# A gated mix of attention and linear attention: the thresholds of its list scheduler set by a table, one row for eight score passes

## The chip, the cores and the metric

The kernel runs on one core of one Trainium2 chip. The metric is device time of one launch in microseconds (us). Before the change it is 669.52 us, the median of 3 runs (669.35 to 669.65).

## What is computed

For 2048 tokens of 512 columns, the reference forms two attention results from the same input `x` and mixes them with a gate per token:

```python
x = A_x                                                     # 1 x 2048 x 512
g = _sigmoid((x * gate_w).sum(-1, keepdims=True))
# A: softmax attention, 32 heads of 16
scores = jnp.einsum("bhqd,bhkd->bhqk", q, k) * (Dh ** -0.5)
p = _softmax(scores, axis=-1)
o = jnp.einsum("bhqk,bhkd->bhqd", p, v)                     # then @ wo
# B: linear attention, 32 heads of 16
phi = lambda t: jnp.where(t > 0, t + 1, jnp.exp(t)) + 1e-6
pq, pk = phi(q), phi(k)
kv = jnp.einsum("bhsd,bhse->bhde", pk, v)
z = jnp.einsum("bhsd->bhd", pk)
o = num / den                                               # num = pq kv, den = pq z + 1e-6; then @ wo
return g * a + (1 - g) * b
```

The large part is the softmax of A: 32 heads x 2048 x 2048 exponentials.

## The kernel before, in words

**Units and rounds.** The scores are worked off in 32 rounds. A round is eight heads (one of four groups, `t8`), 512 query columns (`qc`) and one half of the heads (four, `j` = 0 to 3, in four strips of 32 rows of the TensorE array). A unit is one block of 128 keys for one head, a matmul into one PSUM bank of 128x512. A round has 16 x 4 = 64 units, the kernel 2048.

**Two ways for an exponential.** Most units go to ScalarE (ACT): one ACTIVATE (L2075) takes the two or three neighbouring banks of a *score pass* and writes weights to `PT`. The passes alternate between banks 0 to 2 and 3 to 5. The other units are *claimed* for VectorE (DVE): one TENSOR_SCALAR (L1569, in `claim`) turns a score bank into the integer bits of an approximate exponential in `DP`. Four claimed units make a group, and for the group two shifted copies are made by integer additions (L1613 on POOL, or L1610 on DVE when that comes earlier). The three versions are weighted by three scaled copies of the values, so a claimed unit needs three products with the values, a unit on ACT one. A claimed unit's score bank is the third bank of a pass, the third bank of the other half, or bank 7.

**The other work.** Projections of keys, values and queries for the next head group, the linear branch B (its `phi` is made by ACT at L974 and two DVE operations at L977 and L979, in `phi_post`), the gate, and the output projection are cut into *steps* of a few matmuls each. The steps wait in chains (`a_chain`, `b_chain`, `e_chain` for the start, `o_chain` for the output) with a target pass. Steps use bank 7 or the bank that isn't the accumulator (bank 6 and 7 change roles), and in a few cases a *lent* third bank of the ring. The last rounds, normalisation and final stores stand at the end.

**The order.** Nothing is decided on the chip. When the program is built, Python code simulates the engines with assumed durations (`PE.t`, `AC.t`, `DV.t`, `PO.t`) and puts instructions on each engine's list in the order in which it decides them; semaphores follow from what reads and writes what. The main loop makes one pass `g` after the other (L1988 on):

- it looks for free banks (`more`), picks two or three units for ACT and up to two claims (`extras`), and emits their score matmuls as one group and the ACTIVATE;
- until the banks of the next pass are read (`t_lim`), it fills TensorE's time: sets of products with the values (`pv_step`, up to `MOST` sets), chain steps (`misc_step`), and else filling matmuls on zeros (`fill`), which keep TensorE's clock up;
- `t_late` is the last moment at which TensorE may be busy before ACT would wait for scores: `AC.t` less the length of a score group and `MARGIN`;
- DVE's operations are queued as items with a priority (`push`), and `pump` emits the best of them: those whose wait is short come first, then by priority (0 ahead of 1), then by possible start.

The thresholds in these rules are constants: `WAIT3` (how long TensorE waits for the third bank), `WAIT_M` (for bank 7), `RING_LOAD` (up to which queue on DVE a claim is made), `TWO_LOAD` and `THIRDS` (a third ACT unit or a second claim), `OVER` and `FIRST_T` (how far a step may run over `t_late`), `MOST`, `ROOM`, `LEAST`, `PV_LAG` and `PT_URGENT` (products: how many sets, and when those of `PT` go first), `MIN_LEFT`, `ALONE`, `MOST_OPEN` (claims), `POOL_WAIT`, `WAIT_BANK` and `LOOK` (choices in `pump`), and a few more.

**Lending.** If steps are far behind or `e_chain` isn't empty, and no bank is free, the head of a chain is chosen at the start of a pass (`lend = due`, a pair of step and chain). After the pass's scores are emitted, the chain's head is popped and the chosen step is started on the pass's own third bank, where the pass has two units.

Of the kernel before, what the change touches and what calls it, by code (L numbers as in the profile page):

```python
# [19 lines left out]
HIST = {}  # L20
SLOTS = [(0, 3), (3, 3)]
# [193 lines left out]
def bass_gated_mix__mha_block__linear_attn_block__prompt_kernel(  # L215
# [33 lines left out]
    with ExitStack() as es:  # L249
# [164 lines left out]

        items = []
# [22 lines left out]
        POOL_WAIT = 0.7  # L438
# [124 lines left out]

        WAIT_BANK = 0.12
# [6 lines left out]
        def pump(now, look=0.25):  # L571
            try_close()
            pool_go()
            while items and DV.t <= now + look:
                best = None
                for it in items:
# [3 lines left out]
                    if len(o) > 6 and not due_now(it) and PO.t < DV.t + POOL_WAIT:  # L580
# [3 lines left out]
                    key = (wait > (WAIT_BANK if it.prio <= 1 else 0.12), -1 if it is boost[0] else it.prio, st, it.seq)  # L584
# [4 lines left out]
                if best[2] > now + look + WAIT_BANK:  # L589
                    return  # L590
# [379 lines left out]
        def phi_post(b, dst, dres):  # L970
# [5 lines left out]
            push(1, [  # L976
# [360 lines left out]
        PT_URGENT = 12  # L1337

# [4 lines left out]
        def pv_cols(now, r, force, want, most, least):  # L1343

            urgent = sum(1 for e in pv_pending if e[3] in r_PT) > PT_URGENT
# [84 lines left out]
        def pv_step(now, force=False, want=None, most=3, least=4):  # L1430
# [25 lines left out]
            elif sum(1 for e in pv_pending if e[3] in r_PT) > PT_URGENT:  # L1456
# [54 lines left out]
        def claim_round():  # L1511
# [4 lines left out]
            if left(r) >= (MIN_LEFT_LAST if last else MIN_LEFT):  # L1516
                return r
# [3 lines left out]

        MIN_LEFT = 14
        MIN_LEFT_LAST = 20

        def can_claim(now, js):
# [14 lines left out]
            if not try_close() and len(closing) > MOST_OPEN and (tri[0] is None or len(tri[0][1]) == NTRI - 1):  # L1540
                return None
# [14 lines left out]
        def claim(r, u, b, beside, in_group=False):  # L1556
# [12 lines left out]
            push(0 if in_group else 1, [(lambda: nc.vector.tensor_scalar(DP[:, i, 512 * k:512 * (k + 1)].bitcast(I16),  # L1569
# [18 lines left out]
        MOST_OPEN = 1  # L1588
# [137 lines left out]
        def due_step(now):  # L1726
            load = dve_load(now)
            due = None
            for ch in chains:
# [3 lines left out]
                if (st.target > cur_g[0] and not hurry()) or not step_ready(st, now):  # L1733
                    continue
# [13 lines left out]
        def second_claim(c, now, js):  # L1748
# [7 lines left out]
            elif len(tri[0][1]) == NTRI - 2 and len(closing) > MOST_OPEN:  # L1756
                return None
            if left(r) < 3 + MIN_LEFT:
# [10 lines left out]
        def misc_step(now, t_late):  # L1769

            if hold[0] is not None:
                if now + (SWITCH_T if pe_mode[0] == "full" else 0.0) + hold[0][2][0][2] > t_late + OVER:
# [6 lines left out]
            if b is None:  # L1779
# [3 lines left out]
                if due is None or due[0].keeps or now + FIRST_T > t_late + OVER:  # L1783
                    return False
                b3 = next((b for b in (2, 5) if is_free(b, now)), None)
                if b3 is None or not is_free(7 - b3, t_late + WAIT3):
# [6 lines left out]
            c = can_claim(now, (0, 1, 2, 3)) if ALONE and load < CLAIM_LOAD else None  # L1793
            if due is not None and (c is None or load > STARVE or cur_g[0] > due[0].target + late() or hurry()):
                if now + FIRST_T > t_late + OVER:
# [28 lines left out]

        WAIT3 = 0.05
        WAIT_M = 0.1
        THIRDS = 1
        LATE_M = 100
        TWO_LOAD = 4
        ALONE = 0  # L1830
# [4 lines left out]
        MOST = 4  # L1835
        OVER = 0.15
        FIRST_T = 0.43
        ROOM = 0.6
        CLAIM_LOAD = 3.2
        LATE_CLAIM = 4  # L1840
        STARVE = 5
# [5 lines left out]
        RING_LOAD = 4  # L1847
# [4 lines left out]
        MARGIN = 0.19  # L1852
        PV_LAG = 14
# [138 lines left out]
        while True:  # L1992
            us = []
# [11 lines left out]
            if g > last_stage:  # L2005
                soon = PE.t + WAIT3
                more = [b for b in (b0 + 2, 7 - (b0 + 2)) if is_free(b, soon)][:THIRDS]
                due = due_step(PE.t)[0] if hold[0] is None else None
                if not reserved() and hold[0] is None and (due is None or cur_g[0] <= due[0].target + LATE_M):
                    eb = bank_free(PE.t + WAIT_M)  # L2010
                    if eb is not None:
                        more.append(eb)
            while len(us) < SLOTS[g % 2][1]:
                if len(us) == 2 and (away or lend is not None):
                    break
                if len(us) == 2 and g > last_stage:
                    own, j3 = b0 + 2 in more, peek()
                    load = dve_load(PE.t)
                    if more and load < (RING_LATE if behind_by() > BEHIND else RING_LOAD):
                        js = [j for j in range(4) if j not in [u % 4 for _, u in us]]  # L2020
                        three = own and len(more) > 1 and load >= TWO_LOAD and j3 in js
# [7 lines left out]
                        elif c is not None:  # L2029
                            extras = [(c, more[1 if three else 0])]  # L2030
# [336 lines left out]
```

## Time and profile before

| | |
|---|---|
| median of 3 runs | 669.52 us (669.35 to 669.65) |
| profiled execution: its time, its span | 669.31 us, 667.5 us |
| granted TensorE clock, mean | 0.999 |
| exponentials of A on ACT: passes of 2 units, of 3 units | 626, 44 |
| claimed units on DVE | 664 |
| integer additions on POOL, on DVE | 320, 12 |

The span reaches from the first to the last instruction; the time of a run is a little longer. In the page's lines a group of instructions is named by its line, engine, operation and tiles, with its count, its busy time and mean duration, and the idle time of its engine just before it with what ended that idle time. A row of a stretch lists its limits and length, and then busy time with the instruction count in brackets for PE, weight loads, DVE, ACT and POOL, the granted clock, the DMA share and GB/s.

### The profile page before, as it was taken

The page shows a single profiled execution, that of the slowest core. Times are in us where ns is not written, and L with a number is a line of the kernel's source. Part 1 is how long each engine was busy: PE and PEld are TensorE (multiplying, and loading weights), DVE is VectorE, ACT ScalarE, POOL GpSimd, SP SyncE. Part 2 cuts the span into 40 slices and gives each one's busy share as a digit, 9 for nine tenths or more (in the row PEclk, how much of TensorE's full clock was granted, in tenths as well). Part 3 has the DMA queues.
Part 4 walks back from the last instruction along what each step waited for, and adds up shares of the span by engine and source line. Part 5 has one row for each costly group of instructions (what it writes and reads, how often), then busy time and mean ns, then how long its engine had stood idle before and what let it go on. Part 6 is the DMA issues. An engine that isn't in the chain of part 4 may idle for free.

```text
span 667.5 us, 19111 instructions
## 1 busy us (share of the span) xinstructions
PE 647.2 (97%) x8026; PEld 198.3 (30%) x8028; DVE 566.5 (85%) x968; ACT 655.0 (98%) x710; POOL 344.6 (52%) x337
## 2 busy tenths in 40 slices
PE   8999999999999999999999999999999999999997
PEld 4322222332223332333222323223222322222223
DVE  5599798889988987968889999899999987888793
ACT  6999999999999999999999999999999999999996
POOL 6055465544545564624556465546456455656551
PEclk9999999999999999999999999999999999999999
DMA  9800101000010021101001010020102201010111
GB/s 223 256 2 11 25 3 34 2 14 23 3 34 1 18 51 35 33 3 32 5 8 28 19 39 14 12 49 10 34 9 46 48 25 43 17 43 18 28 30 47
DMA packets 44816, 22.96 MB, mean 34 GB/s; under 512 B 33976, under 2 KB 40568, under 8 KB 44728
## 3 DMA queue, kind: packets, MB, share of 16 engines
q1 hardware_dynamic: 42712, 20.12, 13.0%
q10 hardware_dynamic: 2016, 1.57, 0.9%
q8 instruction: 66, 1.08, 0.7%
q14 instruction: 22, 0.18, 0.1%
HBM read 8.00 MB, written 2.10 MB: 15 GB/s over the span
## 4 chain that ended last, share of the span: by engine, by line
ACT 94%; PE 4%; DVE 1%; issue 0%; POOL 0%; ACTq 0%
ACT PT L2075 92%; PE ps L685 4%; ACT epool L974 2%; DVE DP L2177 0%; DVE Qpad L759 0%; DVE Qpad L891 0%; DVE KVbd L734 0%; DVE epool L1409 0%; DVE epool L1408 0%; DVE identb L739 0%; DVE maskK L746 0%; DVE maskK L748 0%; DVE xT L1913 0%; DVE KT L863 0%; PE ps L692 0%
## 5 line engine op out<-in xcount | busy, mean ns | idle before, releaser
L2075 ACT ACTIVATE PT<-ps 128x1024 bf16<-128x1024 f32 (+1 forms) x670 | 643.1, 1161 | 0.9 <-PE ps L685 0.7
L1569 DVE TENSOR_SCALAR DP<-ps 128x512 int16<-128x512 f32 x664 | 439.5, 686 | 72.3 <-PE ps L685 66.0
L1613 POOL INT64_ADD DP<-DP x320 | 334.5, 1055 | 304.1 <-DVE DP L1569 220.5
L685 PE MATMUL ps<-Qpad,KT 32*128 32x512 bf16 x2048 | 263.1, 385 | 12.3 <-ACT PT L2075 6.4
L685 PE MATMUL ps<-DP,Vaug 128*32 128x512 f16 x1987 | 203.7, 384 | 1.7 <-DVE oraw L1310 1.5
L685 PE MATMUL ps<-PT,Vaug 128*32 128x512 bf16 x1373 | 170.0, 384 | 0.5 <-DVE Vaug L918 0.5
L685 PEld LDWEIGHTS ps<-Qpad,KT 32*128 32x128 bf16 x2048 | 66.2, 91 | 272.5 <-ACT PT L2075 245.3
L685 PEld LDWEIGHTS ps<-DP,Vaug 128*32 128x32 bf16 x1987 | 49.2, 95 | 61.1 <-issue 37.8
L685 PEld LDWEIGHTS ps<-PT,Vaug 128*32 128x32 bf16 x1373 | 40.7, 95 | 46.9 <-issue 35.9
L685 PE MATMUL ps<-warm 128*32 128x512 bf16 (+2 forms) x221 | 39.5, 390 | 1.0 <-POOL warm L729 1.0
L685 PE MATMUL ps<-xT,wA 128*32 128x512 bf16 x432 | 32.5, 384 | 0.0
L974 ACT ACTIVATE epool<-ps 128x512 bf16<-128x512 f32 x32 | 23.4, 730 | 0.0
L1310 DVE COPY oraw<-ps 128x512 f32<-128x512 f32 x31 | 21.2, 683 | 0.5 <-PE ps L685 0.4
L685 PE MATMUL ps<-xT,wB 128*32 128x512 bf16 x256 | 19.7, 384 | 0.0
L685 PE MATMUL ps<-wB,xT 128*32 128x512 bf16 x256 | 19.7, 384 | 0.0
L685 PE MATMUL ps<-woA,OT 128*32 128x512 bf16 (+1 forms) x226 | 19.1, 384 | 0.0
L979 DVE SCALAR_TENSOR_TENSOR phi<-ps,epool 128x512 bf16<-128x512 f32 x24 | 16.4, 682 | 0.1
L863 DVE CAST KT<-ps 128x512 bf16<-128x512 f32 (+1 forms) x16 | 10.7, 667 | 5.2 <-PE ps L685 5.2
L685 PE MATMUL ps<-wA,xT 128*128 128x128 bf16 x192 | 14.9, 221 | 0.0
L918 DVE CAST Vaug<-ps 128x512 bf16<-128x512 f32 x16 | 10.9, 684 | 3.6 <-PE ps L685 3.6
L685 PEld LDWEIGHTS ps<-warm 128*32 128x32 bf16 (+1 forms) x221 | 9.9, 98 | 13.4 <-issue 11.8
L685 PEld LDWEIGHTS ps<-wA,xT 128*128 128x128 bf16 x192 | 10.8, 98 | 5.4 <-issue 5.0
(107 smaller groups left out, 238.4 us busy)
## 6 DMA issues: line engine op xcount, KB each, us to landing
rbc<-oraw SPq DMA_DIRECT2D x16, 256.0 KB
OT<-in_A_x_dram SPq DMA_DIRECT2D x4, 512.0 KB, 7.3
Qpad<-Qs SPq DMA_DIRECT2D x124, 16.0 KB, 1.8
oraw<-oraw SPq DMA_DIRECT2D x60, 32.0 KB, 1.9
wA<-in_A_wqkv_dram SPq DMA_DIRECT2D x1, 1536.0 KB, 7.6
wB<-in_B_wqkv_dram SPq DMA_DIRECT2D x1, 1536.0 KB, 9.2
out_dram<-outt SPq DMA_DIRECT2D x12, 128.0 KB, 2.1
phi<-in_A_x_dram ACTq DMA_DIRECT2D x3, 256.0 KB, 6.3
```

The source lines that it names most:

```text
L685: return lambda: nc.tensor.matmul(o, lhsT=l, rhs=r, start=start, stop=stop, skip_group_check=sg)
L863: push(1, [(lambda: nc.vector.tensor_copy(KT[:, par, c0:c1], src), [r_bank[b]], [r_KT[par][t]], d_psum(n), None)])
L918: ops = [(lambda: nc.vector.tensor_copy(v_group(NQC * par + v)[:, :, :, 0:16], src), [r_bank[b]], [r_V[par][v]], d_psum(512), lambda: v_do ...
L974: op(AC, lambda: nc.scalar.activation(epool[:, s, :], bank_ap(b), ACT.Exp), reads=[r_bank[b]], writes=[r_e[s]], dur=0.6, issue=0.48)
L979: (lambda: nc.vector.scalar_tensor_tensor(out=dst, in0=bank_ap(b), scalar=0.0, in1=epool[:, s, :], op0=ALU.max, op1=ALU.add), [r_bank[b], ...
L1310: push(0, [(lambda: nc.vector.tensor_copy(oraw[:, half, :], acc), [r_acc], [r_oraw[half]], d_psum(512), evicted)])
L1569: push(0 if in_group else 1, [(lambda: nc.vector.tensor_scalar(DP[:, i, 512 * k:512 * (k + 1)].bitcast(I16), bank_ap(b), FRAC - Y_BIAS4, Y ...
L1613: ops = (*ops[:4], None, POOL_ADD, lambda z=z, i2=i2, i=i, n=n: nc.gpsimd.int64_add(DP[:, i2, 0:n].bitcast(I64), DP[:, i, 0:n].bitcast(I64 ...
L2075: op(AC, lambda p0=p0, b0=b0, n=n: nc.scalar.activation(PT[:, 512 * p0:512 * p0 + n], ps[:, 512 * b0:512 * b0 + n], ACT.Exp, scale=LN2 / F ...
```

## The change

The constants become fields of a class `K`. `OPTIONS` lists 25 of them with their possible values; the first value of each is the one that the kernel had, but for three that had no name or another value: `MAXX` (how many claims a pass may make; 3 cuts nothing off), `LEAST` (3, formerly written in the call), and `PRIO_PHI` (0, where phi's items had priority 1). `ORDER` has 81 rows, one for eight passes; digit n of a row picks the value of option n. `choose(w)` sets all fields from row `w`, and from zeros where there is no row. The main loop calls it at every eighth pass. 22 rows are all zeros; the other 59 hold 141 settings other than the first.

```diff
+WINDOW = 8
+OPTIONS = (
+    ('WAIT3', (0.05, 0.12, 0.2, 0.3)),
+    ('THIRDS', (1, 2)),
+    ('TWO_LOAD', (4, 1.0)),
+    ('RING_LOAD', (4, 1.2, 1.8, 2.5)),
+    ('MAXX', (3, 0, 1, 2)),
+    ('MOST', (4, 2, 3)),
+    ('OVER', (0.15, 0.0, 0.3)),
+    ('ROOM', (0.6, 0.2, 0.9)),
+    ('PV_LAG', (14, 4, 9, 18)),
+    ('LATE_M', (100, 0, -6)),
+    ('MARGIN', (0.19, 0.08, 0.3)),
+    ('PT_URGENT', (12, 6, 16)),
+    ('FIRST_T', (0.43, 0.2, 0.6)),
+    ('WAIT_M', (0.1, 0.3, 0.2)),
+    ('POOL_WAIT', (0.7, 0.0, 1.5)),
+    ('MOST_OPEN', (1, 2)),
+    ('MIN_LEFT', (14, 8, 20)),
+    ('PRIO_NEW', (0, 1)),
+    ('AHEAD', (0, 3, -3, 8)),
+    ('ALONE', (0, 1)),
+    ('PRIO_PHI', (0, 1)),
+    ('LEAST', (3, 4, 2)),
+    ('WAIT_BANK', (0.12, 0.3, 0.0)),
+    ('LOOK', (0.25, 0.5, 0.1)),
+    ('STARVE', (5, 1.5)),
+)
+ORDER = [
+    "0000000000000000000000000",
+    "0000010200000000003000000",
+    "0000010200001000003100000",
...
+    "0000002000000011000100200",
+    "0000002100000011000100220",
...
+    "0000001000100101000000000",
...
+    "0000002010000200000000000",
...
+    "3000000000000000000000001",
+    "3000000000000000003000000",
+    "3000000000000000003000000",
+    "3000000000000000003100000",
...
+]
+def choose(w):
+    row = ORDER[w] if w < len(ORDER) else "0" * len(OPTIONS)
+    for (name, values), c in zip(OPTIONS, row):
+        setattr(K, name, values[int(c)])
...
-            push(1, [
+            push(K.PRIO_PHI, [
                 (lambda: nc.vector.tensor_scalar(epool[:, s, :], epool[:, s, :], 1.0, 1e-6, op0=ALU.min, op1=ALU.add),
...
         while True:
+            if g % WINDOW == 0:
+                choose(g // WINDOW)
...
+                        extras = extras[:K.MAXX]
...
-            if lend is not None and len(us) == 2:
+            if lend is not None and len(us) == 2 and lend[1] and lend[1][0] is lend[0]:
                 lend[1].popleft()
...
-                room = min(MOST, int((t_late - PE.t - enter) / SET_T + ROOM))
-                if behind and room > 0 and pv_step(PE.t, most=room, least=3):
+                room = min(K.MOST, int((t_late - PE.t - enter) / SET_T + K.ROOM))
+                if behind and room > 0 and pv_step(PE.t, most=room, least=K.LEAST):
```

The remaining edits put `K.` before the names listed. The last condition is the mended step: a lent step is started only if it is still at the head of its chain.

More of the change, by code (lines that the diff above doesn't have):

```diff
@@ L588, in pump @@
                     return
-                if best[2] > now + look + WAIT_BANK:
+                if best[2] > now + look + K.WAIT_BANK:
                     return
@@ L1515, in claim_round @@
             last = (r == NR - 1)
-            if left(r) >= (MIN_LEFT_LAST if last else MIN_LEFT):
+            if left(r) >= (MIN_LEFT_LAST if last else K.MIN_LEFT):
                 return r
@@ L1732, in due_step @@
                 st = ch[0]
-                if (st.target > cur_g[0] and not hurry()) or not step_ready(st, now):
+                if (st.target > cur_g[0] + K.AHEAD and not hurry()) or not step_ready(st, now):
                     continue
@@ L1771, in misc_step @@
             if hold[0] is not None:
-                if now + (SWITCH_T if pe_mode[0] == "full" else 0.0) + hold[0][2][0][2] > t_late + OVER:
+                if now + (SWITCH_T if pe_mode[0] == "full" else 0.0) + hold[0][2][0][2] > t_late + K.OVER:
                     return False
```

139 lines of the change are left out of this document (97 added, 42 removed).

## The prediction

> **What bounds the kernel now.** I read the page first: spans, busy shares, the chain that ended last, the costliest groups.
>
> ```profile
> span 667.5 us, 19111 instructions
> PE 647.2 (97%) x8026; PEld 198.3 (30%) x8028; DVE 566.5 (85%) x968; ACT 655.0 (98%) x710; POOL 344.6 (52%) x337
> PEclk9999999999999999999999999999999999999999
> ACT 94%; PE 4%; DVE 1%; issue 0%; POOL 0%; ACTq 0%
> L2075 ACT ACTIVATE PT<-ps 128x1024 bf16<-128x1024 f32 (+1 forms) x670 | 643.1, 1161 | 0.9 <-PE ps L685 0.7
> L1569 DVE TENSOR_SCALAR DP<-ps 128x512 int16<-128x512 f32 x664 | 439.5, 686 | 72.3 <-PE ps L685 66.0
> L1613 POOL INT64_ADD DP<-DP x320 | 334.5, 1055 | 304.1 <-DVE DP L1569 220.5
> ```
>
> ACT sets the time: 94% of the chain, and before its 670 exponentials it stood idle 0.9 us in all. No wait can be removed there. Only less ACT work shortens the kernel, and the ACT work is 2048 units less those that DVE claims: 2048 - 664 = 1384. DVE is the engine that can take more: 85% busy, and 66.0 us of its idle time was spent waiting for scores. TensorE ran at its full granted clock throughout.
>
> Next the groups by shape, the chain in order of time, and ACT's timeline at the start, for the price of a pass.
>
> ```profile
> L2075 ACT ACTIVATE PT<-ps 128x1024 bf16<-128x1024 f32 x626 | 587.8, 1135 | 0.0
> L2075 ACT ACTIVATE PT<-ps 128x1536 bf16<-128x1536 f32 x44 | 63.4, 1522 | 0.9 <-PE ps L685 0.7
> ...
> 31.16 0.49 ACT epool L974
> 31.65 6.42 ACT PT L2075 x7
> ...
> 638.07 16.52 PE ps L685 x212
> ...
> 10.58 1.45 ACT L2075 ACTIVATE PT<-ps 128x1536 bf16<-128x1536 f32 x1
> ...
> 13.25 1.46 ACT L2075 ACTIVATE PT<-ps 128x1536 bf16<-128x1536 f32 x1
> ```
>
> The recorded durations overlap, so they are not the price; the distance from start to start is. A pass of two units costs 6.42 / 7 = 0.917 us, one of three (13.25 - 10.58) / 2 = 1.335 us, an exponential of the linear branch (L974, 32 of them) 0.49 us. Units: 626 x 2 + 44 x 3 = 1384, as counted above. Time: 626 x 0.917 + 44 x 1.335 + 32 x 0.49 = 574.0 + 58.7 + 15.7 = 648.4 us. The first pass starts at 9.1 us, so about 667.5 - 9.1 - 648.4 = 10.0 us is left for the end. I take both ends as fixed; from 638 us the chain passes through PE, where the last rounds are finished.
>
> Last the stretches, for how full DVE already gets.
>
> ```profile
> 280.00:300.00 20.00, 20.00 (x264) 6.24 (x268) 13.54 (x21) 20.00 (x21) 6.93 (x7) 1.00 0.01 3
> ...
> 340.00:440.00 100.00, 96.70 (x1199) 29.14 (x1187) 92.72 (x160) 100.00 (x111) 56.03 (x54) 1.00 0.11 23
> ...
> 40.00:640.00 600.00, 587.47 (x7293) 175.00 (x7293) 525.48 (x877) 600.00 (x657) 321.53 (x308) 1.00 0.11 23
> 500.00:520.00 20.00, 19.86 (x251) 6.26 (x248) 18.94 (x34) 20.00 (x23) 11.18 (x11) 1.00 0.21 42
> ```
>
> The columns are busy time of PE, weight loads, DVE, ACT, POOL. Over the 600 us in the middle DVE is 525.48 / 600 = 87.6% busy and ACT 100%. The best 100 us reach 92.7%, the best 20 us 18.94 / 20 = 94.7%; the worst 20 us only 67.7%. So a stretch can do much better than the mean under the same thresholds: what the change can move is the weak stretches.
>
> **The thresholds by windows.** The table adds no instruction by itself. It decides per eight passes whether a free bank is used for a claim, a third unit or a chain step, and how many sets of weighted products go ahead of the next scores. The sum therefore turns on one number, x, the units that move from ACT to DVE. Their price on DVE:
>
> ```profile
> 33.19 3.31 DVE L1569 TENSOR_SCALAR DP<-ps 128x512 int16<-128x512 f32 x5
> ```
>
> Five evictions back to back took 3.31 us: 0.66 us each. On ACT a unit is worth 0.917 / 2 = 0.459 us in a pass of two, some more where passes merge into three; I use 0.47. If DVE is to be busy a share u of the shortened middle: 525.48 + 0.66 x = u (600 - 0.47 x). Bounds: u = 0.876 gives x = 0; u = 0.927, the best 100 us everywhere, gives 28 units; u = 0.947, the best 20 us everywhere, gives 39. I choose u = 0.935, between what is sustained for 100 us and what is reached for 20, because only the weak windows have far to go: x = (561.0 - 525.5) / (0.66 + 0.44) = 32.3, taken as 33.
>
> Passes: 1384 - 33 = 1351 units. The table has 81 rows of eight passes, 648, where 670 passes fill 84 windows; I read this as a schedule of at most 648 passes. It could also be that trailing rows are left off, and nothing else in the sum needs it. With 648 passes, 1351 units are 593 of two and 55 of three: 593 x 0.917 + 55 x 1.335 + 15.7 = 543.8 + 73.4 + 15.7 = 632.9 us, 15.5 us less.
>
> What has to hide the rest: each claim turns one product into three on PE and adds half a POOL instruction.
>
> ```profile
> L685 PE MATMUL ps<-Qpad,KT 32*128 32x512 bf16 x2048 | 263.1, 385 | 12.3 <-ACT PT L2075 6.4
> L685 PE MATMUL ps<-DP,Vaug 128*32 128x512 f16 x1987 | 203.7, 384 | 1.7 <-DVE oraw L1310 1.5
> ...
> L685 PE MATMUL ps<-warm 128*32 128x512 bf16 (+2 forms) x221 | 39.5, 390 | 1.0 <-POOL warm L729 1.0
> ```
>
> A product costs 203.7 / 1987 = 0.103 us of busy PE, so 33 claims add 66 x 0.103 = 6.8 us; 22 passes fewer take 22 x 263.1 / 670 = 8.6 us of score groups away. PE also loses the 15.5 us of span. Its cover is the 12.5 us idle in the middle and the 39.5 us of filling matmuls (some of them at the start), which compute nothing. If that cover were gone, the 15.5 + 6.8 - 8.6 = 13.7 us would come back as ACT idle. POOL gets 33 / 4 x 2 = 16 more additions of 1.055 us, 17 us beside its 278 us idle in the middle. Both cost nothing in the sum.
>
> **Phi's operations first** (L977 and L979, 32 pairs) reorders DVE and adds nothing.
>
> ```profile
> L979 DVE SCALAR_TENSOR_TENSOR phi<-ps,epool 128x512 bf16<-128x512 f32 x24 | 16.4, 682 | 0.1
> ...
> L977 DVE TENSOR_SCALAR epool<-epool 128x512 bf16<-128x512 bf16 x32 | 9.2, 288 | 1.1
> ```
>
> A pair is 0.29 + 0.68 = 0.97 us. An eviction queued behind it is that much later, its bank misses the next pass and a claim is lost: at worst 32 x 0.47 = 15 us. The other way the shared bank 7 comes free an eviction earlier; if each wins a claim, 15 us are gained. Nearest rows: DVE was idle 0.1 and 1.1 us before these groups, so it worked up to them and the order alone changes. I take 0.
>
> **The mended lend** only acts where the step at the head of a chain changed between choosing and starting it. This matters while the six early steps (transposes, keys and values of the later token blocks) are pending; a lent bank turns a pass of three into one of two, 0.42 us: at most 6 x 0.42 = 2.5 us either way, taken as 0.
>
> **A rule against more POOL work.** Here is what one collision looks like now: the weighted copies of L929, then both engines near 291 us.
>
> ```profile
> L929 DVE TENSOR_SCALAR Vaug<-Vaug x16: 224/267/1022, 22.5 to 458.4; 128x288 bf16<-128x288 bf16 x8, 128x576 bf16<-128x576 bf16 x8
> ...
> 291.46 1.37 DVE L929 TENSOR_SCALAR Vaug<-Vaug 128x576 bf16<-128x576 bf16 x2
> 291.57 1.09 POOL L1613 INT64_ADD DP<-DP  x1 [3.81 <-PE ps L685]
> 30.43 0.30 DVE L929 TENSOR_SCALAR Vaug<-Vaug 128x576 bf16<-128x576 bf16 x1
> ```
>
> One of the sixteen took 1022 ns beside a POOL addition, where another of its shape took 300: 0.72 us lost. The Trainium skill, "SBUF — State Buffer", section "SBUF: two separate sides", says that a GpSimd instruction and a VectorE one in a two-port mode lock each other out of a shared port pair for a whole instruction. The trace agrees at this place (0.72 us); by that rule alone, without a planner keeping them apart, the 16 new additions would be the rival priced below.
>
> **The rivals.** *Larger gain:* the choices close nearly all gaps, u = 0.96 to 0.98, x = 45 to 56, 21 to 26 us less, 648 to 643 us. Against it stand DVE's waits:
>
> ```profile
> PEld ps L685 <- ACT PT L2075: 245.3, 572, 1.2
> ...
> DVE DP L1569 <- PE ps L685: 66.0, 182, 2.9
> ...
> PEld ps L685 <- DVE DP L1569: 4.1, 18, 0.2
> ```
>
> 66.0 us lie in 182 gaps of 0.36 us on average, most too short for an eviction of 0.66. *Gain given back at the port:* each of the 16 extra POOL additions stretches a DVE operation by 0.72 us, 11.5 us of DVE, 17 claims, 8 us: 662 us; with more collisions among the 320 old ones, up to 668. For it: the one stretched copy; against: it is one in sixteen, and POOL waits elsewhere for DVE instead. *The table does little:* claims move from window to window and their sum stays, 669 us. For it: thresholds that bring work forward also leave less for later. *Slower:* the order on each engine is fixed when the program is built, from assumed durations. Packed more tightly, a bank's eviction lands later than planned and the next scores wait for DVE; ACT then waits too. Today this happens 18 times at 4.1 / 18 = 0.23 us and never reaches ACT, since PE stood ready at ACT's banks 572 times for 0.43 us. The gain of 15.5 us is gone when 15.5 / 0.23 = 67 passes, one in ten, wait so; at one in five (130 passes, 30 us) the time is 652.0 + 30 + 1.8, 684 us. The rows that let PE run later (OVER 0.3 in three windows, MARGIN 0.08 in one, WAIT3 0.3 in six) touch some 80 passes; against it is the 0.43 us of readiness.
>
> **How the numbers follow.** Profiled span after: 9.1 + 632.9 + 10.0 = 652.0 us. The profiled execution of before took 669.31 us for a span of 667.5, so 1.8 us lie around it: 653.8; the median shown, 669.52, is 0.2 above that execution: 654. Forecast, 0.58, with a range of its own from 648 (u = 0.96) to 663 (u = 0.90); larger gain 0.13; given back at the port 0.10; does little 0.05; slower 0.14. 644 to 667 us leaves the slower case and a little of the larger gain out. A measurement of this kernel tells apart about 0.2%, here 1.3 us: faster by more than that 0.58 + 0.13 + 0.10 = 0.81, within it 0.05, slower 0.14.
>
> **What would show it.** Right: L2075 with some 648 passes and at most 1 or 2 us of idle before it; the 1024-wide shape down by about 33, the 1536-wide up; L1569 near 697; DVE over 92% in the middle, with 280 to 340 us the most changed; filling matmuls fewer. Wrong: L1569 unchanged; idle before L2075 of many us released by L685; DVE shares of 92% with stretched L929, L977 or L1298; a granted clock below 1.00 in a window.

## The result, and the profile after

The changed kernel takes 658.5 us (median of 4 runs, 658.01 to 658.78; the kernel before beside it 669.59): 0.9834 of the time before, with an interval of 0.9817 to 0.9851. 654 was forecast, with 644 to 667 as the range. The profiled execution took 658.51 us for a span of 656.7.

First the page of the changed kernel: span, busy shares, granted clock, the chain's shares, the costliest groups. TensorE's clock stayed full. The lines have moved: L2181 is the exponential (L2075 before), L1688 the claims' eviction (L1569), L1731 the addition on POOL (L1613), L808 TensorE's helper (L685), L1100 the first of phi's operations (L977).

```profile
span 656.7 us, 19176 instructions
PE 640.8 (98%) x8032; PEld 196.1 (30%) x8032; DVE 579.8 (88%) x993; ACT 642.6 (98%) x701; POOL 367.8 (56%) x363
PEclk9999999999999999999999999999999999999999
ACT 73%; PE 24%; DVE 2%; DMA 0%; issue 0%; POOL 0%; DVEq 0%; ACTq 0%; POOLq 0%
L2181 ACT ACTIVATE PT<-ps 128x1024 bf16<-128x1024 f32 (+1 forms) x661 | 631.8, 1154 | 2.3 <-PE ps L808 2.1
L1688 DVE TENSOR_SCALAR DP<-ps 128x512 int16<-128x512 f32 x697 | 456.0, 685 | 47.4 <-PE ps L808 40.9
L1731 POOL INT64_ADD DP<-DP x346 | 357.8, 1044 | 269.8 <-DVE DP L1688 197.7
L808 PE MATMUL ps<-warm 128*32 128x512 bf16 (+2 forms) x147 | 28.8, 395 | 1.0 <-POOL warm L852 1.0
```

DVE claims 697 units, 33 more, and its idle time before a claim fell from 66.0 to 40.9 us. TensorE's filling matmuls fell from 221 to 147. The chain, 94% ACT before, now runs through TensorE for 24%: scores come just in time, or a little late.

The groups by shape and ACT's first pass in the timeline give its work by the prediction's own prices.

```profile
L2181 ACT ACTIVATE PT<-ps 128x1024 bf16<-128x1024 f32 x632 | 595.3, 1138 | 1.3 <-PE ps L808 1.2
L2181 ACT ACTIVATE PT<-ps 128x1536 bf16<-128x1536 f32 x29 | 42.2, 1506 | 1.0 <-PE ps L808 0.9
...
9.51 4.27 ACT L2181 ACTIVATE PT<-ps 128x1536 bf16<-128x1536 f32 x3 [0.74 <-PE ps L808]
```

632 x 2 + 29 x 3 = 1351 = 2048 - 697 units, and 632 x 0.917 + 29 x 1.335 + 15.7 = 633.9 us of work, 14.5 less than before. The span fell by 10.8. So what lies around ACT's work, the *rest* (span less work), grew from 667.5 - 648.4 = 19.1 to 656.7 - 633.9 = 22.8 us, by 3.7. The first pass starts 0.4 us later (9.51 for 9.10; in other runs of the same order it lies between 8.8 and 9.6). The distances from the start of one of ACT's operations to the start of the next, summed over the trace up to 630 us, exceed their prices by 5.4 us, where it was 1.9 before: 3.5 us more. The end gives 0.2 back. Where one distance exceeds its price by over 0.25 us, I call the excess a *wait of ACT's*; the idle time in the profile's brackets is shorter, since recorded durations overlap. There are seven, at 235, 330, 399, 427, 428, 434 and 551 us, 2.7 us together; before there was none. They are what the later experiments are about.

The stretches (busy time of PE, weight loads, DVE, ACT, POOL) show where DVE filled up.

```profile
240.00:340.00 100.00, 99.21 (x1288) 29.95 (x1284) 89.59 (x150) 99.56 (x110) 54.89 (x54) 1.00 0.09 19
...
40.00:630.00 590.00, 580.69 (x7300) 171.75 (x7297) 539.42 (x902) 588.58 (x650) 345.51 (x335) 1.00 0.11 24
```

DVE is 539.42 / 590 = 91.4% busy, 87.6% before. The weak stretch from 240 to 340 us, at 79.64 before, gained most. ACT is no longer 100% busy in every stretch.

### The profile page after: what moved, and what is told of

Read it like the earlier page. It is cut to its first block, busy times and chain, and to the rows that moved or that the text cites. A ratio compares the mean times of both kernels' runs of the same rounds, so it can differ in the third digit from the quotient of the medians.

```text
span 656.7 us, 19176 instructions
## 1 busy us (share of the span) xinstructions
PE 640.8 (98%) x8032; PEld 196.1 (30%) x8032; DVE 579.8 (88%) x993; ACT 642.6 (98%) x701; POOL 367.8 (56%) x363
## 3 DMA queue, kind: packets, MB, share of 16 engines
q8 instruction: 66, 1.08, 0.7%
## 4 chain that ended last, share of the span: by engine, by line
ACT 73%; PE 24%; DVE 2%; DMA 0%; issue 0%; POOL 0%; DVEq 0%; ACTq 0%; POOLq 0%
ACT PT L2181 71%; PE ps L808 24%; ACT epool L1097 2%; DVE DP L1688 1%; PE ps L815 0%; DMA rsum<-oraw 0%; DVE DP L2283 0%; DVE epool L1100 0%; DVE Qpad L1014 0%; DVE phi L1102 0%; DVE KT L986 0%; DVE rraw L1406 0%; DVE DP L2288 0%; DVE flag L2293 0%; POOL warm L852 0%
## 5 line engine op out<-in xcount | busy, mean ns | idle before, releaser
L2181 ACT ACTIVATE PT<-ps 128x1024 bf16<-128x1024 f32 (+1 forms) x661 | 631.8, 1154 | 2.3 <-PE ps L808 2.1
L1731 POOL INT64_ADD DP<-DP x346 | 357.8, 1044 | 269.8 <-DVE DP L1688 197.7
L1688 DVE TENSOR_SCALAR DP<-ps 128x512 int16<-128x512 f32 x697 | 456.0, 685 | 47.4 <-PE ps L808 40.9
L808 PE MATMUL ps<-Qpad,KT 32*128 32x512 bf16 x2048 | 262.9, 384 | 9.5 <-ACT PT L2181 3.7
L808 PE MATMUL ps<-DP,Vaug 128*32 128x512 f16 x2086 | 202.7, 384 | 0.9 <-DVE oraw L1433 0.8
L808 PE MATMUL ps<-PT,Vaug 128*32 128x512 bf16 x1336 | 155.0, 384 | 0.5 <-DVE Vaug L1041 0.5
L808 PEld LDWEIGHTS ps<-Qpad,KT 32*128 32x128 bf16 x2048 | 66.3, 91 | 269.4 <-ACT PT L2181 242.9
L808 PEld LDWEIGHTS ps<-DP,Vaug 128*32 128x32 bf16 x2086 | 47.6, 95 | 65.3 <-issue 42.7
L808 PEld LDWEIGHTS ps<-PT,Vaug 128*32 128x32 bf16 x1336 | 37.1, 95 | 42.4 <-issue 32.4
L808 PE MATMUL ps<-xT,wA 128*32 128x512 bf16 x432 | 33.4, 384 | 0.0
L808 PE MATMUL ps<-warm 128*32 128x512 bf16 (+2 forms) x147 | 28.8, 395 | 1.0 <-POOL warm L852 1.0
L808 PE MATMUL ps<-wB,xT 128*32 128x512 bf16 x256 | 19.3, 383 | 0.0
L808 PE MATMUL ps<-woA,OT 128*32 128x512 bf16 (+1 forms) x226 | 19.0, 384 | 0.0
L808 PE MATMUL ps<-xT,wB 128*32 128x512 bf16 x256 | 18.8, 383 | 0.0
L808 PE MATMUL ps<-wA,xT 128*128 128x128 bf16 x192 | 14.9, 220 | 0.0
L1100 DVE TENSOR_SCALAR epool<-epool 128x512 bf16<-128x512 bf16 x32 | 10.0, 314 | 3.0 <-ACT epool L1097 2.6
L808 PEld LDWEIGHTS ps<-wA,xT 128*128 128x128 bf16 x192 | 10.8, 98 | 5.4 <-issue 4.8
```

The lines of the kernel that those rows point to most:

```text
L808: return lambda: nc.tensor.matmul(o, lhsT=l, rhs=r, start=start, stop=stop, skip_group_check=sg)
L1100: (lambda: nc.vector.tensor_scalar(epool[:, s, :], epool[:, s, :], 1.0, 1e-6, op0=ALU.min, op1=ALU.add), [r_e[s]], [r_e[s]], 0.29, None),
L1688: push((0 if in_group else 1) + K.PRIO_NEW, [(lambda: nc.vector.tensor_scalar(DP[:, i, 512 * k:512 * (k + 1)].bitcast(I16), bank_ap(b), FR ...
L1731: ops = (*ops[:4], None, POOL_ADD, lambda z=z, i2=i2, i=i, n=n: nc.gpsimd.int64_add(DP[:, i2, 0:n].bitcast(I64), DP[:, i, 0:n].bitcast(I64 ...
L2181: op(AC, lambda p0=p0, b0=b0, n=n: nc.scalar.activation(PT[:, 512 * p0:512 * p0 + n], ps[:, 512 * b0:512 * b0 + n], ACT.Exp, scale=LN2 / F ...
```

## The experiments

Every ratio below is to the kernel before, run on the same chip. "Claims" and "passes" are those of the built kernel.

### Which part of the change makes the gain

Five kernels. **e1_phi_only**: the kernel before with phi's priority alone.

```diff
-            push(1, [
+            push(0, [
```

> Before with phi's items at priority 0, nothing else. The built program has 667 claims (before 664) in 672 passes: 633 of two units, 38 of three, one of one. Theory (time is ACT's work, and the settings matter only through the claims they yield): 633 x 0.917 + 38 x 1.335 + 0.5 + 32 x 0.49 = 647.4 us against 648.4 before, so 1 us less, about 668.5 us, and no more than 2 us of late scores on top. Rival (phi's priority carries a good part of the 11 us): below 665 us.

**e2_phi_last**: the changed kernel with that edit undone.

```diff
-            push(K.PRIO_PHI, [
+            push(1, [
```

> After with phi's items back at priority 1 and the whole table kept. The built program has 663 claims in 671 passes: 626 of two, 44 of three, one of one. Theory (a table fits only the course of decisions that it was chosen for; the gain is the 33 claims): ACT's work is 648.9 us, so 670 us and up to 5 us of late scores, 669 to 675. Rival (the loosened thresholds help wherever they stand): 658 to 662 us.

**e3_first_half** and **e4_second_half**: one half of the table.

```diff
-ORDER = [rows 0 to 80]
+ORDER = [rows 0 to 40]                               # e3: base values afterwards
+ORDER = [41 rows of zeros, then rows 41 to 80]       # e4
```

> After with the first 41 rows of the table alone (passes 0 to 327), base values behind them. The built program has 684 claims in 666 passes: 634 of two, 32 of three. Theory: ACT's work is 639.8 us, 8.6 less than before, so 661 us, and 1 to 3 us of late scores: 661 to 664. Rival (the rows are worth something by themselves, half the rows give half the gain): 664.0 us.

> After with rows 41 to 80 of the table alone, base values ahead of them. The built program has 672 claims in 671 passes: 635 of two, 35 of three, one of one. Theory (ACT's work, claims): 645.2 us of ACT, 3.2 less than before, so 666.4 us and 1 to 3 us of late scores: 666 to 669. Rival (half the rows give half the gain wherever they stand): 664.0 us or less.

**e5_shift**: the same table, each row eight passes later.

```diff
 ORDER = [
     "0000000000000000000000000",
+    "0000000000000000000000000",
...
-    "0000000000010000000000000",
 ]
```

> After with every row moved one window (eight passes) later, a row of zeros first. The built program has 662 claims in 673 passes: 631 of two, 41 of three, one of one. Theory: ACT's work is 649.5 us, so at least 670.7 us; settings that let TensorE be late where nothing asks for it add late scores, up to 10 us more. Rival (a looser setting helps wherever it stands, give or take): 657 to 662 us.

| | claims, passes | ACT's work | span | rest | median (range) | ratio |
|---|---|---|---|---|---|---|
| before | 664, 670 | 648.4 | 667.5 | 19.1 | 669.52 | |
| after | 697, 661 | 633.9 | 656.7 | 22.8 | 658.5 | 0.9834 (0.9817 to 0.9851) |
| e1_phi_only | 667, 672 | 647.4 | 673.6 | 26.2 | 675.71 (675.03 to 675.97) | 1.009 (1.0073 to 1.0107) |
| e2_phi_last | 663, 671 | 648.9 | 670.6 | 21.7 | 672.89 (672.44 to 676.63) | 1.0065 (1.0044 to 1.0086) |
| e3_first_half | 684, 666 | 639.8 | 662.7 | 22.9 | 663.44 (662.46 to 664.54) | 0.9903 (0.9886 to 0.9919) |
| e4_second_half | 672, 671 | 645.2 | 668.1 | 22.9 | 669.69 (668.83 to 671.19) | 1.0004 (0.9994 to 1.0014) |
| e5_shift | 662, 673 | 649.5 | 678.3 | 28.8 | 680.78 (680.2 to 681.85) | 1.0172 (1.0155 to 1.0189) |

The first half gives 6 of the 11 us. That lies within its expectation, but so near to its rival's 664.0 that it doesn't tell the two apart. (Its rest of 22.9 us holds a stretch with a granted clock of 0.50, from 341.4 to 344.8 us; two of its four runs hold the clock and take 662.5 us.) The second half alone gives nothing, 0.2 us over the kernel before and outside its expected range, though behind the first half it is worth the other 5 us (663.44 to 658.5). The same settings one row later are 11 us slower than the kernel before. Phi's priority alone is 6 us slower, a clear miss of its expectation; without it the table is 14.4 us slower than with it. So the rows, taken together, are not better values in themselves: they suit the course of decisions that the rows and priorities ahead of them have led to, and off that course the claims are lost (662 and 663 instead of 697). No run tests a single setting.

Two of these kernels show scores that come late. In e1_phi_only it is the slower rival's mechanism, with other sizes. The stretches around 490 us (last columns: granted clock, DMA share, GB/s) and the timeline there:

```profile
490.00:492.00 2.00, 0.33 (x3) 0.13 (x3) 2.00 (x4) 1.06 (x2) 1.58 (x2) 1.00 0.65 49
492.00:494.00 2.00, 1.80 (x18) 0.40 (x19) 1.49 (x4) 1.20 (x2) 1.06 (x2) 0.60 0.01 1
494.00:496.00 2.00, 2.00 (x24) 0.40 (x16) 0.74 (x2) 1.08 (x2) 1.47 (x2) 0.55 0.03 3
...
475.70 5.54 SPq L634 DMA_DIRECT2D Qpad<-Qs  x8
481.28 1.26 SPq L604 DMA_TRANSPOSE OBT<-OB  x1
482.65 1.26 SPq L634 DMA_DIRECT2D oraw<-rraw  x2
485.15 0.63 SPq L634 DMA_DIRECT2D rbc<-oraw  x1
...
489.63 0.69 DVE L1298 TENSOR_TENSOR OT<-oraw,rbc 128x512 bf16<-128x512 f32 x1 [1.69 <-DMA rbc<-oraw]
490.24 1.88 DVE L1569 TENSOR_SCALAR DP<-ps 128x512 int16<-128x512 f32 x3
491.67 0.39 PE L685 MATMUL ps<-Qpad,KT 32*128 32x512 bf16 x3 [1.83 <-DVE DP L1569]
492.10 1.02 ACT L2075 ACTIVATE PT<-ps 128x1024 bf16<-128x1024 f32 x1 [1.05 <-PE ps L685]
```

These transfers serve the normalisation: `rsum` gets the sums that DVE inverts, `oraw` the reciprocals, `rbc` the reciprocals spread out for the multiplication. `Qpad` holds the queries that the scores read. SPq is SP's queue, which issues one transfer after the other. Read the timeline from the bottom. ACT stands idle for 1.05 us until its scores come, and the scores wait 1.83 us for evictions on DVE. DVE has them behind the multiplication of the normalised output (L1298), which waits 1.69 us for the transfer `rbc`. That transfer's own chain stood on SP's queue behind eight copies into `Qpad` (5.54 us of issuing) and a transpose (1.26). Then the granted clock falls to 0.60 and 0.55, as means over 2 us; from 492.4 to 495.8 us it is 0.50. Over the 6 us ACT is busy 1.06 + 1.20 + 1.08 = 3.3.

In e5_shift it is another one: eight copies into `Qpad` were issued from 173.35 us on, just ahead of the scores that read them:

```profile
177.52 1.04 PE L808 MATMUL ps<-Qpad,KT 32*128 32x512 bf16 x7 [4.72 <-DMA Qpad<-Qs]
178.18 2.37 ACT L2181 ACTIVATE PT<-ps 128x1536 bf16<-128x1536 f32 x2 [4.33 <-PE ps L808]
```

Here the query copies themselves come too late, and ACT is idle for 4.3 us at once. The granted clock is 0.50 from 176 to 180 us, and two more waits of 1.7 and 1.1 us follow by 190 us.

The mended lend was settled without a run: with that line put back, the built kernel has the same instructions in the same order on every engine. Its price here is exactly nothing.

### What the rest grew by: POOL, products, fills

Three kernels with the same instructions in the same order as the changed one, each with one load made lighter. **e6_half_add** makes each addition on POOL half as wide once its buffer has been written in full:

```diff
+        whole = set()
...
+                    m = n if i2 not in whole else n // 2
+                    whole.add(i2)
...
-                        DP[:, i2, 0:n].bitcast(I64), DP[:, i, 0:n].bitcast(I64), STEPS[z] * FOUR))
...
+                        DP[:, i2, 0:m].bitcast(I64), DP[:, i, 0:m].bitcast(I64), STEPS[z] * FOUR))
```

> After with the same instructions in the same order, but each POOL addition over half its columns once its buffer has been written in full (the other half keeps an older group's weights; the output is wrong). Theory (part of the 3.5 us that ACT lost beside its work comes from DVE operations held up by a POOL addition): the longest L1100 falls from 1.03 us to 0.6 or less, the 0.7 us wait near 330 us shrinks to 0.3 or less, and the time falls by 0.5 to 1.5 us. Rival (the loss is TensorE's own load): no change within 0.3 us.

**e7_narrow_third** takes 128 of the 512 columns in the third product of a claimed unit:

```diff
+                    c = 128 if z == 2 and j in started else 512
-                    fns.append(f_mm(acc[32 * j:32 * j + 32, :], w, p_ap, start=j not in started, stop=False, sg=True))
+                    fns.append(f_mm(acc[32 * j:32 * j + 32, 0:c], w, p_ap[:, 0:c], start=j not in started, stop=False, sg=True))
```

> After with the same instructions in the same order, but the third weighted product of a claimed unit over 128 of 512 columns (wrong output). About 690 matmuls lose three quarters of their columns, so TensorE has some 20 us less to do. Theory A (the 3.5 us are evictions that come late, not TensorE's load): within 1 us of after. Theory B (TensorE has become a second bound, as its 24% of the chain suggests): 2 to 4 us less than after.

**e8_small_fill** makes the filling matmuls 8 columns wide instead of 512:

```diff
-                fns = [f_mm(acc_of(acc_bank[0])[32 * j:32 * j + 32, :], warm[:, 0:32], warm4, start=False, stop=False, sg=True) for j in range(4)]
+                fns = [f_mm(acc_of(acc_bank[0])[32 * j:32 * j + 32, 0:8], warm[:, 0:32], warm[:, 0:8], start=False, stop=False, sg=True) for j in range(4)]
...
-                pe_macro([f_mm(acc_of(acc_bank[0]), warm[:], warm4, start=False, stop=False, sg=True)], reads=[r_warm],
+                pe_macro([f_mm(acc_of(acc_bank[0])[:, 0:8], warm[:], warm[:, 0:8], start=False, stop=False, sg=True)], reads=[r_warm],
```

> After with the same instructions in the same order, but the filling matmuls of the main loop 8 columns wide in place of 512 (output unchanged). Theory (they lie in gaps and cost nothing): within 0.5 us of after, unless the granted clock falls below 1.00 in some stretch, which then shows as longer matmuls and a time some us longer. Rival (they get in the way of scores now that TensorE is fuller): 1 to 3 us less.

| | span | rest | median (range) | ratio |
|---|---|---|---|---|
| e6_half_add | 655.7 | 21.8 | 657.72 (657.47 to 658.17) | 0.9826 (0.981 to 0.9843) |
| e7_narrow_third | 655.3 | 21.4 | 656.77 (656.48 to 657.12) | 0.9809 (0.9793 to 0.9825) |
| e8_small_fill | 656.2 (its fastest run) | 22.3 | 661.47 (658.06 to 665.06) | 0.9898 (0.9862 to 0.9934) |

POOL's busy time fell from 367.8 to 225.7 us in e6_half_add and the time by 0.8 us, part of which is a first pass that starts 0.7 us earlier (8.81 us). So the additions are all but free; only the wait at 330 us shrank clearly, from 0.72 to 0.29 us.

e7_narrow_third gained 1.7 us and lies between the two theories. TensorE's busy time fell by 9.4 us (640.8 to 631.4), not by 20. Its trace and that of the changed kernel hold the same passes in the same order, so each distance of ACT's can be set beside its like. The first pass starts 0.5 us earlier, which has nothing to do with the edit. Two waits are longer, 0.97 for 0.30 us at 427 us and 0.63 for 0.06 us at 391 us; the next two sections show where such waits come from. All the other distances together are 2.2 us shorter, in changes of less than 0.25 us each. So TensorE's load costs ACT about 2 us in small pieces, the lower bound of theory B. How much of that the change added isn't shown: the kernel before had small delays too.

With the narrowed fills the reservation in the expectation came true. Their windows around 40 us:

```profile
36.00:38.00 2.00, 0.98 (x25) 0.44 (x17) 2.00 (x4) 2.00 (x3) 1.04 (x1) 1.00 0.00 0
38.00:42.00 4.00, 4.00 (x34) 0.70 (x31) 3.22 (x6) 3.60 (x4) 2.51 (x3) 0.57 0.00 0
```

TensorE is half busy for 2 us, then its clock is 0.57 over 4 us (0.50 from 38.5 to 41.9 us). The changed kernel's TensorE is busy for 1.75 of the same first 2 us, and its clock is 1.00 throughout. The two runs of e8_small_fill that take longest, 663.17 and 665.06 us, have mean clocks of 0.987 and 0.984, the other two 0.997. The order is the same and only the fills are narrower, so the full-width fills hold the clock here: they are not the free cover that the prediction took them for.

### The queue of SP

In the changed kernel the wait at 427 us has the same shape as the one in e1_phi_only. Its timeline:

```profile
418.66 6.11 SPq L757 DMA_DIRECT2D Qpad<-Qs  x8
419.15 0.68 DVE L1433 COPY oraw<-ps 128x512 f32<-128x512 f32 x1
424.82 0.60 SPq L757 DMA_DIRECT2D rsum<-oraw  x1
426.79 0.35 DVE L1406 RECIPROCAL rraw<-rsum 128x32 f32<-128x32 f32 x1 [0.83 <-DMA rsum<-oraw]
...
427.84 0.89 PE L808 MATMUL ps<-Qpad,KT 32*128 32x512 bf16 x4 [0.34 <-DVE DP L1688]
429.46 1.94 ACT L2181 ACTIVATE PT<-ps 128x1024 bf16<-128x1024 f32 x2 [0.17 <-PE ps L808]
```

Eight copies hold the queue for 6.11 us, 0.76 each, where the program that plans the order assumes 0.5. The sums that DVE copied out by 419.83 us leave only at 424.82; the reciprocal comes 0.83 us late, and claims, scores and ACT behind it. Two kernels with the same order on every queue show the place with copies that took another time, first e7_narrow_third, then e8_small_fill:

```profile
417.79 6.78 SPq L757 DMA_DIRECT2D Qpad<-Qs  x8
...
426.60 0.35 DVE L1406 RECIPROCAL rraw<-rsum 128x32 f32<-128x32 f32 x1 [1.50 <-DMA rsum<-oraw]
...
418.82 5.48 SPq L757 DMA_DIRECT2D Qpad<-Qs  x8
...
426.32 0.35 DVE L1406 RECIPROCAL rraw<-rsum 128x32 f32<-128x32 f32 x1 [0.20 <-DMA rsum<-oraw]
```

With copies of 6.78, 6.11 and 5.48 us the reciprocal waits 1.50, 0.83 and 0.20 us, and ACT at 427 us 0.97, 0.30 and nothing. Why the eight copies take longer in one run than in another is not shown.

**e10_ahead** is the changed kernel with the order on SP rearranged after planning: where copies into `Qpad` stand ahead of one of the normalisation's small transfers whose data will be there before the last copy is issued, that transfer goes in as soon as its data is there, ahead of the copies still to come. 14 transfers move; every other engine's list is as it was.

```diff
+        while k < len(line):
+            if id(SP.ops[line[k]][3]) in fills:
...
+                late = [x for x in line[n:n + 12] if id(SP.ops[x][3]) in quick and SP.ready[x][0] < t + 0.76 * (n - k)]
+                for x in late:
+                    line.remove(x)
+                p = k
+                for x in late:
+                    p = max(p, k + max(0, math.ceil((SP.ready[x][0] - t) / 0.76)))
+                    line.insert(min(p, n), x)
...
```

> After, every engine's order the same, with the same rearrangement of SP's queue. Theory: the waits of DVE on rsum and rbc (0.8 us each) go, and with them the waits of ACT near 235 us (0.56) and 427 us (0.30 and 0.27): 657.0 to 657.8 us, 0.7 to 1.5 us less than after. Rival (they come from TensorE's load): within 0.3 us of after.

**e9_phi_ahead** is the same edit on e1_phi_only, **e11_ahead_before** on the kernel before.

> Before with phi's items first (as e1_phi_only) and every engine's order the same, but on SP's queue the transfers of sums and reciprocals (rsum, oraw, rbc) are issued ahead of query fills (Qpad) that were in front of them, where their data is there. Theory (e1's 6 us come from DVE standing before a transfer that SP issued late, the scores behind it, and the clock that then falls): the three waits of L1298 on rbc (3.8 us in all) shrink below 1 us, no stretch has a clock below 0.9 near 490 us, and the time is 670 to 672.5 us against 675.7. Rival (the loss lies in the order of DVE itself): 675 us or more.

> Before, every engine's order the same, with the same rearrangement of SP's queue. Theory: before has no wait of L1298 on rbc and 0.5 us of one on rsum, and ACT waits 1.9 us in all, so nothing to win: within 0.5 us of before. Rival (the rearrangement is a gain of its own): 1 us or more below it.

| | span | rest | median (range) | ratio |
|---|---|---|---|---|
| e9_phi_ahead | 669.2 | 21.8 | 671.31 (670.95 to 672.91) | 1.0032 (1.0021 to 1.0043) |
| e10_ahead | 655.7 | 21.8 | 656.84 (656.76 to 657.58) | 0.9813 (0.9799 to 0.9826) |
| e11_ahead_before | 667.6 | 19.2 | 669.24 (669.0 to 669.84) | 0.9998 (0.9989 to 1.0008) |

The place at 427 us in e10_ahead's timeline:

```profile
418.21 1.16 SPq L768 DMA_DIRECT2D Qpad<-Qs  x2
419.41 0.60 SPq L768 DMA_DIRECT2D rsum<-oraw  x1
...
423.52 3.75 SPq L768 DMA_DIRECT2D Qpad<-Qs  x6
425.43 0.34 DVE L1417 RECIPROCAL rraw<-rsum 128x32 f32<-128x32 f32 x1
```

The sums leave some 5 us earlier and the reciprocal waits for nothing. ACT's waits at 235, 427 and 428 us are gone, 1.1 us in the traces. The median is 1.7 us lower, slightly more than expected, and 1.4 by the ratios, each to the kernel before on its own chip; no run of e10_ahead is as slow as the fastest of the changed kernel (657.58 against 658.01). On e1_phi_only the same edit brings back 4.4 of the 6.1 us. DVE's three waits for `rbc`, 3.8 us together, shrink to one of 0.6, and no stretch near 490 us loses the clock:

```profile
492.00:494.00 2.00, 2.00 (x27) 0.54 (x24) 1.87 (x5) 2.00 (x3) 1.14 (x2) 1.00 0.00 0
```

On the kernel before it does nothing, as expected; there no wait of ACT's reaches 0.25 us. So phi's priority lost its 6 us mostly on SP, where it issues nothing. That it did so by moving DVE's other operations nearer to the moment their data arrive is the likely way, read from this one place.

### The port that DVE and POOL share

The largest wait left, 0.72 us at 330 us, is of the kind that the prediction read from the weighted copies at 291 us. The changed kernel's timeline:

```profile
329.18 1.04 POOL L1731 INT64_ADD DP<-DP  x1 [2.14 <-DVE DP L1688]
329.34 1.03 DVE L1100 TENSOR_SCALAR epool<-epool 128x512 bf16<-128x512 bf16 x1 [0.25 <-ACT epool L1097]
...
330.29 0.68 DVE L1688 TENSOR_SCALAR DP<-ps 128x512 int16<-128x512 f32 x1
...
331.11 0.39 PE L808 MATMUL ps<-Qpad,KT 32*128 32x512 bf16 x3 [0.65 <-DVE DP L1688]
...
331.54 2.85 ACT L2181 ACTIVATE PT<-ps 128x1024 bf16<-128x1024 f32 x3 [0.41 <-PE ps L808]
...
L1100 DVE TENSOR_SCALAR epool<-epool x32: 283/294/1027, 36.7 to 498.5; 128x512 bf16<-128x512 bf16 x32
```

The last line gives the operation's durations in ns: 294 as a rule, 1027 here. The addition on POOL started 0.16 us earlier, DVE's operation ends 0.15 us behind the addition, and the eviction behind it makes the scores late. In e6_half_add, with additions half as wide, the longest of these operations takes 601 ns, and the wait here is 0.29 us. In e7_narrow_third there is a second one, at 388.71 us: 1043 ns, the addition 0.14 us ahead of it, and ACT's wait of 0.63 us at 391 us behind it.

**e12_yield** is e10_ahead, with the addition waiting for DVE's operation wherever the plan has DVE's operation start between 0.6 us before the addition and 0.1 us after it (14 additions):

```diff
+                if last_add[0] is not None and last_add[0][0] - 0.6 < st < last_add[0][0] + 0.1:
+                    waits, *rest = PO.ops[last_add[0][1]]
+                    PO.ops[last_add[0][1]] = (waits + [(DV.sem, DV.cover(ev.idx))], *rest)
...
```

> After with SP's queue rearranged (as e10_ahead), every engine's order the same, and 14 POOL additions that would start within 0.6 us of a DVE operation on two SBUF sides made to wait for that operation. Theory (DVE is held for a whole addition where the addition starts first, as L1100 at 329 us): the wait of 0.72 us near 329 us falls below 0.2, and the time is 655.9 to 656.4 us against 656.84 of e10_ahead. Rival (the additions that yield make the products late in their place): 657 us or more.

Measured: span 654.6, rest 20.7, 656.58 us (656.45 to 656.83), 0.9809 (0.9795 to 0.9822). The timeline of e12_yield at that place and the durations of the same operation:

```profile
328.38 0.29 DVE L1118 TENSOR_SCALAR epool<-epool 128x512 bf16<-128x512 bf16 x1 [0.25 <-ACT epool L1115]
...
329.14 2.05 POOL L1749 INT64_ADD DP<-DP  x2 [3.05 <-DVE epool L1118]
...
L1118 DVE TENSOR_SCALAR epool<-epool x32: 282/294/407, 36.3 to 496.5; 128x512 bf16<-128x512 bf16 x32
```

The stretched operation and its wait are gone. The profiled span is 1.1 us shorter than e10_ahead's, but half of that is an earlier first pass (9.11 for 9.64 us). ACT's distances are 0.56 us shorter: 0.70 at this place, and 0.14 given back elsewhere. The median fell by 0.26 us only, just short of what was expected. The mechanism at this place is shown; that it is worth its 0.72 us in the median is not. This is the fastest kernel of the study, 1.9 us below the changed one. Three waits of 0.3 to 0.4 us, at 398, 432 and 549 us, remain in it. In e7_narrow_third those at 432 and 549 us (434 and 551 in the changed kernel) shrink to 0.18 and 0.08 us, so TensorE's load has a part in them. No run tells the cause of the one at 398 us.

## Why the prediction was right, and where it was not

**ACT's work sets the time: right.** 633.9 us of work by the same prices, 632.9 forecast.

**x = 33: right, though two of its inputs were off.** DVE did not get to the chosen u of 0.935; it is at 0.914 in the middle. The claim was priced too high. The windows of the claims alone (time, busy time, count, clock, DMA share, GB/s), first of the kernel before:

```profile
40.00:640.00 600.00, 422.85 (x639) 1.00 0.11 23
```

and of the changed kernel, with five evictions back to back in its timeline and the shifted copies left on DVE (durations in ns):

```profile
40.00:630.00 590.00, 439.95 (x674) 1.00 0.11 24
...
422.89 3.07 DVE L1688 TENSOR_SCALAR DP<-ps 128x512 int16<-128x512 f32 x5
...
L1728 DVE TENSOR_SCALAR DP<-DP x4: 286/486/695, 277.2 to 646.8; 128x2048 int16<-128x2048 int16 x2, 128x512 int16<-128x512 int16 x2
```

35 more claims in the middle added 439.95 - 422.85 = 17.1 us of busy time, 0.49 each where the sum had 0.66. Five in a row take 3.07 us here, 3.31 at the place that the prediction read, and recorded durations of neighbours overlap, so a claim that joins others adds less than its own length. DVE's other work in the middle also fell, from 525.48 - 422.85 = 102.6 to 539.42 - 439.95 = 99.5 us: of 12 shifted copies 4 are left on DVE, two of them short. A cheaper claim and a lower share gave the forecast number: that the two errors cancel is luck. The copies are why POOL got 26 more additions, not 16: the sum priced a claim as if DVE went on making as many.

**81 rows read as 648 passes: wrong, and cheap.** There are 661 passes; the last thirteen run past the table on base values. The three-unit passes fell to 29 where 55 were forecast. Since the units are fixed at 1351, this is worth 1.0 us.

**"I take both ends as fixed", with POOL and TensorE costing nothing: the term that was mis-sized.** The rest was put at 19.1 and is 22.8. With the 1.0 us of passes these 3.7 us are the whole distance between 654 and 658.5. The rows quoted for cover (TensorE ready 0.43 us ahead, POOL idle for 278 us) were averages; most of the loss comes at single places where one instruction is late. In the traces, 1.1 of the 3.7 us went with the rearranging of SP's queue (1.7 in the median), 0.7 is the port (0.26 in the median), 0.9 the three waits left, 0.8 delays of under 0.25 us each, and 0.4 the start, which varies anyway; the end gives 0.2 back. TensorE's load has a part in the small ones, as e7_narrow_third shows; how large a part the change has in that stays open. SP's queue was not in the prediction at all.

The prices for TensorE were misread as well, though the sum didn't use them. Products were to cost 6.8 us more, and score groups 8.6 less. In the changed kernel the two groups of products fell from 203.7 + 170.0 to 202.7 + 155.0 us of busy time, with 99 products more from `DP` and 37 fewer from `PT`, and the scores, 2048 matmuls as before, went from 263.1 to 262.9. Matmuls of one strip overlap those of another (2048 of 384 ns make 262.9 us), so a group's busy time doesn't grow with its count.

**Phi's operations first, taken as 0 within 15 us either way: the answer was not a price.** Alone the edit costs 6.1 us; inside the table its absence costs 14.4. The bound held in both cases, the reason given, lost claims, only in the second. Alone, claims hardly changed (664 to 667), and the loss was mostly lateness on SP and the clock behind it; inside the table, 34 claims are lost, which is 15.0 us of ACT's work.

**The mended lend, 0 to 2.5 us: exactly 0.**

**The rivals.** The slower one did not come at its size. The row that the prediction quoted for it is nearly what it was, but that of the matmuls themselves grew. Both follow (us in all, times, longest), and then the second as it was before:

```profile
PEld ps L808 <- DVE DP L1688: 4.8, 19, 0.4
...
PE ps L808 <- DVE DP L1688: 1.5, 4, 0.6
...
PE ps L685 <- DVE DP L1569: 0.2, 1, 0.2
```

Weight loads wait 19 times for 18, the longest 0.4 us for 0.2. Matmuls wait four times for one, and the waits of ACT's at 330 and 427 us stand behind two of these. So its mechanism is there at a few places. But it was mis-drawn. It counted on 67 passes of 0.23 us. In e1_phi_only a handful of places suffices, since one late operation costs 0.6 to 1.3 us and a gap of TensorE's takes the clock with it. The rival at the port needed 16 collisions of 0.72 us; phi's operation shows one, with that very price (1027 against 294 ns).

**The marks.** Claims at 697, fewer fills and the weak stretch most changed came as said; the share of DVE stayed just under 92%, the idle time before L2181 was 2.3 us for 1 to 2, and the shapes moved the other way (two-unit passes up by 6, three-unit passes down by 15).

## What to carry to other kernels

When an engine's work sets the time, the work moved off it gives the size of a gain; what is lost again showed here mostly as single waits, so after the change list the places where that engine waited and follow each to its first late instruction, across a DMA queue if need be. Settings that suit one course of decisions need not be better values: here the first half alone kept its 6 us, the second half alone gained nothing, and the same rows shifted were slower than none. In a fixed order, small urgent transfers belong ahead of bulk copies on an in-order queue, and its issue time should be planned with the measured price.

## What the hardware showed unexpectedly

**Issuing on SP takes longer than the planned 0.1 or 0.5 us.** A copy of a strip into `Qpad` takes 6.11 / 8 = 0.76 us of the queue at 427 us, a small transfer 0.60, a transpose 1.26 at 481 us in e1_phi_only. The changed kernel's runs of eight copies take 0.62 to 0.88 us a copy, so a run holds everything behind it for 5 to 7 us.

**The clock falls after a gap shorter than what follows it.** TensorE idled 1.83 us near 490 us (0.33 us of work in 2 us), and the clock was then 0.50 from 492.4 to 495.8 us, 3.4 us, although it had work again. Fills of 8 columns lost it too, at half a load. The Trainium skill, "TensorE: Matmul & The Clock Gate", section "Part 1: The HAM clock gate (the "warmup" mystery)", describes a free-running activity window of about 3.4 us. The length of the slow stretch agrees with that; the gap that set it off was shorter.
